# Fewer, longer loads of the combined weights, and two kinds of small transfers moved to GpSimd's queue

## The chip, the core and the metric

The kernel runs on one core of a Trainium2 chip. The metric is the device time of one execution in microseconds (us). Before the change the median of three runs is 834.39 us (834.20 to 834.68).

## What is computed

Eight batches of 576 tokens with eight heads of 64 numbers go through attention inside chunks of 64 tokens, and the 4608 token rows of 512 numbers that come out go through a feed-forward layer with an ELU between its two matrices. Everything is in 32-bit floats.

```python
scores = scale * np.matmul(q_c, k_c.transpose(0, 1, 2, 4, 3))   # chunks of 64
attn = softmax(scores);  out = np.matmul(attn, v_c)
x = out.transpose(0, 2, 1, 3).reshape(B * S, H * D)             # 4608 x 512
h = x @ w_in                                                    # w_in 512 x 2048
g = np.where(h > 0.0, h, np.exp(np.minimum(h, 0.0)) - 1.0)
return g @ w_out                                                # w_out 2048 x 512
```

## The kernel before

**Precision.** An operand is split in a high and a low part, and a product is three matmuls (`three`, L431): high by high, high by low, low by high. Nearly all of PE's time is such 128x512 matmuls at L434.

**Blocks.** The tokens are nine blocks of 512. Blocks 0 to 2 are plain: for each of 16 slices `f` of w_in the first layer (`hidden`), the ELU, the split of its result into `ghi` (ACT) and `glo` (L479, in block 2, the third, on GpSimd), and the second layer. The other six are three superblocks of two blocks, which are multiplied by a scheme of seven products in place of eight. It needs sums and differences of quarters of the weights. Superblock 0 is written out by hand; superblocks 1 and 2 are laid in an order by `Plan`, a list scheduler in the kernel that knows for each job an engine, a time that the engine is occupied, a time until its result can be used, and what it reads and writes.

**Where the combined weights come from.** Those of w_in are made in the second block by `combine` (L512): GpSimd adds, ACT and DVE split, and SP's queue writes the parts to `a_dram` (L536, L537 and L547). Those of w_out are made by the class `Sums` (L564) in eight pieces `j`: GpSimd or DVE adds, ACT makes the high part (`high`), GpSimd or DVE the low one (`low`), and four transfers of 256 KB for each `j` go to `w_dram` (`write_half`, L601). Pieces 4 and 5 are made in the third block (strings such as `w4g` in `MORE_THIRD`; letters g to j are the writes), 0, 3 and 1 in superblock 0, and 2, 6 and 7 (`LATE_SUMS`) at the start of superblock 1.

**The ring.** In superblocks 1 and 2, PE reads the combined weights from a ring of four slots of 512 KB. `load_entry` (L1302) fills a slot when PE is done with the entry four places earlier. A superblock has 28 entries from `a_dram` (its first phase: products with w_in) and then 28 from `w_dram` (second phase). An entry from `a_dram` is two transfers of 256 KB (L1308) in pieces of 1 KB, one from `w_dram` is one transfer of 512 KB (L1313) in pieces of 4 KB. PE uses an entry for two steps of six matmuls. Superblock 0 loads from `a_dram` too (`load_a`, L671).

**Attention beside it.** While a block is multiplied, the attention of a later block is made, one tile of 128 tokens after another. For a tile, PE multiplies q by k (L248, into `ps_a`), DVE and ACT make the softmax, DVE turns blocks of 32x32 (`turned`, L388), ACT copies that to `unturned` (L393), and four transfers of 32 KB exchange the off-diagonal blocks: `swap_turned` (L399) writes parts of `unturned` back into `turned`. Then PE multiplies by v (L256). PE works in order, so a late exchange holds all of its matmuls. Below, an exchange is these four transfers.

**Queues.** Every transfer is issued by SP, in program order: an instruction that waits for its semaphore, or for room in the queue, holds all behind it. GpSimd issues none; it also works in order.

## Time and profile before

| what | value |
|---|---|
| median of three runs | 834.39 us |
| the profiled execution | 837.23 us |
| its span | 835.5 us |
| PE busy | 811.7 us, 97% |
| DVE, ACT, GpSimd busy | 612.4, 523.6 and 165.9 us |
| share of the 16 DMA engines | 77.3%, mean 230 GB/s |
| packets under 2 KB | 195696 of 214335 |

The span is what the trace covers; the profiled execution's own time is 1.7 us longer. Every time on a row counts from the span's start. The profile names a group of instructions by line, engine, operation and tiles (`out<-in`); SPq is SP's queue, and its rows say how long SP took to issue, not how long a transfer ran. "Idle before" in square brackets tells how long the engine stood before a row and who ended that. PE's rows overlap in print, as matmuls are pipelined: what counts is the distance from start to start. Groups of twelve matmuls in stride stand 2.72 us apart.

Stages of the span: plain blocks to about 324 us (the third one from about 233 us), superblock 0 to 506 us, superblock 1 from 506 to 676 us (its first phase to 595 us), superblock 2 from 676 us to the end.

### The profile page before, as it was taken

How to read it: one execution, taken by the hardware profiler on the slowest of the kernel's cores; microseconds unless marked ns; L12 is line 12 of the kernel's file. 1: busy time of each engine (PE TensorE's matmuls, PEld its weight loads, DVE VectorE, ACT ScalarE, POOL GpSimd, SP SyncE). 2: the span in 40 equal slices, each digit the busy share in tenths (PEclk: the TensorE clock that was granted, in tenths of full speed). 3: DMA queues.
4: the chain of work that ended last, by engine and by line, in shares of the span. 5: the costliest groups of instructions: out<-in, count | busy, mean ns of one | idle time of the engine just before them, and what ended most of it. 6: DMA issues, size and time to landing. Idle time of an engine off the chain costs nothing.

```text
span 835.5 us, 15987 instructions
## 1 busy us (share of the span) xinstructions
PE 811.7 (97%) x5853; PEld 660.3 (79%) x5853; DVE 612.4 (73%) x915; ACT 523.6 (63%) x990; POOL 165.9 (20%) x140
## 2 busy tenths in 40 slices
PE   7899999999999989999999999998999999999997
PEld 6688788888878868877888888776788878888886
DVE  4999997666875739766556866867789966557974
ACT  4999875454554535765566445886877736776451
POOL 0000014355335411443111253100020010000100
PEclk8999999999999989999999999999999999999999
DMA  8975764987887887679987898999966587665655
GB/s 232 271 226 192 236 195 138 288 251 252 266 218 212 234 235 196 204 223 252 289 238 216 250 266 284 282 279 265 292 210 204 200 220 228 196 190 197 210 198 152
DMA packets 214335, 191.93 MB, mean 230 GB/s; under 512 B 85616, under 2 KB 195696, under 8 KB 214256
## 3 DMA queue, kind: packets, MB, share of 16 engines
q1 hardware_dynamic: 214256, 190.90, 77.3%
q8 instruction: 47, 0.77, 0.4%
q14 instruction: 32, 0.26, 0.1%
HBM read 144.18 MB, written 42.99 MB: 224 GB/s over the span
## 4 chain that ended last, share of the span: by engine, by line
PE 76%; DMA 8%; ACT 5%; DVE 4%; SPq 4%; issue 2%; POOL 1%; DVEq 0%; POOLq 0%; ACTq 0%
PE o L434 37%; PE h L434 32%; PE ps_a L248 2%; PE ps_a L256 2%; DMA turned<-unturned 2%; DMA ring<-a_dram 2%; DMA kept<-in_q_dram 1%; PE h L451 1%; DMA v_sb<-in_v_dram 1%; SPq L1308 1%; ACT ps_a L1562 1%; DMA g_kept<-lo_dram 1%; SPq L206 1%; DMA ring<-w_dram 1%; DMA q_sb<-in_q_dram 1%
## 5 line engine op out<-in xcount | busy, mean ns | idle before, releaser
L434 PE MATMUL o<-wo_hi,ghi 128*128 128x512 f32 x272 | 108.8, 400 | 0.0
L434 PE MATMUL o<-wo_hi,glo 128*128 128x512 f32 x272 | 107.2, 394 | 0.1
L434 PE MATMUL o<-wo_lo,ghi 128*128 128x512 f32 x272 | 107.1, 394 | 0.0
L434 PE MATMUL h<-xhi,wi_hi 128*128 128x512 f32 x228 | 84.0, 397 | 0.1
L434 PE MATMUL h<-xlo,wi_hi 128*128 128x512 f32 x228 | 82.4, 390 | 0.0
L434 PE MATMUL h<-xhi,wi_lo 128*128 128x512 f32 x180 | 70.3, 390 | 0.0
L434 PEld LDWEIGHTS o<-wo_hi,glo 128*128 128x128 f32 x272 | 51.7, 190 | 11.8 <-DVE glo L479 0.8
L434 PEld LDWEIGHTS o<-wo_hi,ghi 128*128 128x128 f32 x272 | 51.6, 190 | 11.4
L434 PEld LDWEIGHTS o<-wo_lo,ghi 128*128 128x128 f32 x272 | 51.7, 190 | 10.3
L510 POOL TENSOR_TENSOR kept<-wi_hi,wi_lo 128x512 f32<-128x512 f32 x16 | 21.3, 1348 | 158.4 <-DMA kept<-in_k_dram 117.3
L471 DVE SCALAR_TENSOR_TENSOR e<-e,h 128x512 f32<-128x512 f32 x48 | 32.9, 685 | 26.9 <-ACT e L469 26.6
L434 PE MATMUL o<-split,ring 128*128 128x512 f32 x216 | 51.0, 390 | 0.0
L434 PEld LDWEIGHTS h<-xhi,wi_hi 128*128 128x128 f32 x228 | 42.7, 188 | 9.9 <-ACT kept L783 0.7
L434 PEld LDWEIGHTS h<-xlo,wi_hi 128*128 128x128 f32 x228 | 42.9, 188 | 8.5
L434 PEld LDWEIGHTS o<-split,ring 128*128 128x128 f32 x216 | 40.5, 188 | 8.4
L393 ACT COPY unturned<-turned 128x512 f32<-128x512 f32 x28 | 17.4, 622 | 46.7 <-DVE turned L388 45.9
L468 ACT ACTIVATE e<-h 128x512 f32<-128x512 f32 x48 | 28.6, 597 | 28.7 <-PE h L434 26.1
L476 ACT CAST ghi<-e 128x512 fp32r<-128x512 f32 x48 | 29.8, 621 | 18.7 <-DVE e L471 18.6
L434 PE MATMUL h<-split,ring 128*128 128x512 f32 x168 | 40.5, 393 | 0.5 <-DMA ring<-w_dram 0.5
L744 POOL TENSOR_TENSOR glo<-e,ghi 128x512 fp32r<-128x512 f32 x16 | 20.7, 1293 | 99.0 <-ACT ghi L742 99.0
L1488 ACT ACTIVATE e<-e 128x512 f32<-128x512 f32 x64 | 39.5, 630 | 1.0
L434 PEld LDWEIGHTS h<-xhi,wi_lo 128*128 128x128 f32 x180 | 33.8, 188 | 7.1
(224 smaller groups left out, 2014.1 us busy)
## 6 DMA issues: line engine op xcount, KB each, us to landing
ring<-a_dram SPq DMA_DIRECT2D x112, 256.0 KB, 3.9
ring<-w_dram SPq DMA_DIRECT2D x56, 512.0 KB, 3.3
wi_hi<-a_dram SPq DMA_DIRECT2D x56, 256.0 KB, 5.4
kept<-in_q_dram SPq DMA_DIRECT2D x100, 128.0 KB, 3.4
kept<-in_k_dram SPq DMA_DIRECT2D x100, 128.0 KB, 3.9
wo_lo<-lo_dram SPq DMA_DIRECT2D x20, 512.0 KB, 6.1
v_sb<-in_v_dram SPq DMA_DIRECT2D x32, 256.0 KB, 5.4
st<-in_moe_w_in_dram SPq DMA_DIRECT2D x16, 512.0 KB, 4.0
```

Of the source, the lines that this page charges most:

```text
L206: nc.sync.dma_start(out=dst[p0:p0 + n], in_=src[b, :, s0:s0 + n, :].rearrange("h s d -> s h d"))
L248: nc.tensor.matmul(scores[halves[c], j, hp, :], lhsT=qT[halves[j], hp, halves[c]], rhs=kT[halves[j], hp, halves[c]], start=True, stop=True,)
L256: nc.tensor.matmul(x_ps[halves[j], c, hp, :], lhsT=v_sb[halves[c], 2 * hp + j, :], rhs=aT[halves[c], :, j * NK + hp], start=True, stop=True,)
L393: nc.scalar.copy(out=unturned, in_=turned)
L434: nc.tensor.matmul(ps, lhsT=a, rhs=b, start=start, stop=stop, skip_group_check=onto)
L451: nc.tensor.matmul(h, lhsT=w[:, kt, :], rhs=x[:, kt, :], start=i == 0, stop=i == len(terms) - 1)
L468: nc.scalar.activation(out=e, in_=h, func=AF.Relu, scale=-1.0)
L471: nc.vector.scalar_tensor_tensor(out=e, in0=e, scalar=-1.0, in1=h, op0=ALU.add, op1=ALU.max)
L476: nc.scalar.copy(out=ghi, in_=e)
L510: nc.gpsimd.tensor_tensor(out=out, in0=a, in1=b, op=op)
L744: engine.tensor_tensor(out=lo, in0=e, in1=hi.bitcast(F32), op=ALU.subtract)
L1488: nc.scalar.activation(out=units[u], in_=units[u], func=AF.Exp, scale=-1.0)
```

## The change

- `a_dram` is laid out anew, by operand and pair of pieces. An entry of the ring is now one transfer of 512 KB in pieces of 4 KB (56 transfers in place of 112), and a load in superblock 0 has pieces of 2 KB in place of 1 KB. In return `write_parts` issues three transfers of 128 KB in place of one of 256 KB and one of 128 KB (16 more transfers in all), and the pieces of `write_sums` are 1 KB in place of 4 KB.
- The writes of `Sums` pieces 4 and 5 (third block) and 6 and 7 (superblock 1), sixteen transfers of 256 KB, are issued by GpSimd in place of SP. The others stay with SP.
- In the planned part, which is superblock 1, the exchanges are issued by GpSimd: seven of them, 28 transfers. The exchanges of all earlier blocks stay with SP.
- The planner gets a further engine "QUEUE" for what GpSimd issues, with costs of its own, and does not count it as GpSimd's time; `LATE_SUMS` starts pieces 6 and 7 earlier.

```diff
-        def swap_turned(self):
+        def swap_turned(self, queue=nc.sync):
...
-                    nc.sync.dma_start(out=turned[to, 1 - e], in_=unturned[of, e])
+                    queue.dma_start(out=turned[to, 1 - e], in_=unturned[of, e])
...
-    a_dram = dram.tile([NG, P, 2, NA, 2 * P], F32, name="a_dram")
+    a_dram = dram.tile([NA, NG // 2, P, 2, 2, 2 * P], F32, name="a_dram")
...
-            nc.sync.dma_start(out=rows(g, lo)[:, :4], in_=w1.bitcast(F32))
-            nc.sync.dma_start(out=rows(g, lo)[:, 4:6], in_=w2[:, 2:].bitcast(F32))
+            for i, w in enumerate((w1[:, :2], w1[:, 2:], w2[:, 2:])):
+                nc.sync.dma_start(out=rows(i, g, lo), in_=w.bitcast(F32))
...
-                nc.sync.dma_start(out=rows(g, lo)[:, 6:], in_=place_of(g)[:, lo])
+                nc.sync.dma_start(
+                    out=a_dram[3:, g // 2, :, g % 2, lo, :].rearrange("i p w -> p i w"),
+                    in_=place_of(g)[:, lo].rearrange("p (i k) f -> p i (k f)", k=2))
...
-            sums.write_half(lo, half)
+            sums.write_half(lo, half, nc.gpsimd if preparing == "third" else nc.sync)
...
-            for a in range(2):
-                nc.sync.dma_start(
-                    out=slot[:, a].bitcast(F32),
-                    in_=a_dram[2 * d + a, :, :, AOPS.index(PRODUCTS[FIRST[o]][0])])
+            of = a_dram[AOPS.index(PRODUCTS[FIRST[o]][0]), d]
...
+        nc.sync.dma_start(out=slot.bitcast(F32), in_=of)
...
-    LATE_SUMS = (2, 0), (6, 6), (7, 18)
+    LATE_SUMS = (2, 0), (6, 5), (7, 11)
...
-        plan.add(t + 4.7, "SP", dma(4, 420), lambda: later[n].swap_turned(), ["unturned"], ["turned"])
+        plan.add(t + 4.7, "QUEUE", (2400, 4600), lambda: later[n].swap_turned(nc.gpsimd), ["unturned"], ["turned"])
...
+            if early:
+                plan.add(t + .9 + .5 * i, "SP", dma(1, 800), lambda i=i: made[0].write_half(i // 2, i % 2), *keys)
+            else:
+                plan.add(t + 1.5 + 4 * i, "QUEUE", (2400, 5000),
+                         lambda i=i: made[0].write_half(i // 2, i % 2, nc.gpsimd), *keys)
```

**SP in the third block**, from one exchange to the next (the second is the one at 288.56 us of the profile). Before:

```order
L399 DMA turned<-unturned 32x256 x4
L671 DMA wi_hi<-a_dram 128x2x256 x2
L227 DMA kept<-in_q_dram 32x4x256 x4
L227 DMA kept<-in_k_dram 32x4x256 x4
L601 DMA w_dram<-io 128x2x256
L687 DMA wo_lo<-lo_dram 128x1024
L671 DMA wi_hi<-a_dram 128x2x256 x2
L601 DMA w_dram<-io 128x2x256
L206 DMA v_sb<-in_v_dram 128x8x64
L399 DMA turned<-unturned 32x256 x4
```

After:

```order
L399 DMA turned<-unturned 32x256 x4
L673 DMA wi_hi<-a_dram 128x512 x2
L227 DMA kept<-in_q_dram 32x4x256 x4
L227 DMA kept<-in_k_dram 32x4x256 x4
L689 DMA wo_lo<-lo_dram 128x1024
L673 DMA wi_hi<-a_dram 128x512 x2
L206 DMA v_sb<-in_v_dram 128x8x64
L399 DMA turned<-unturned 32x256 x4
```

The two writes of `io` (piece 4's sums, issued at 284.94 and 287.12 us) that stood between the exchanges are gone from SP. On GpSimd each now stands directly behind a `glo`, those that ran at 272.71 and 278.07 us before, with no loads in front of it.

**SP in the first phase of superblock 1**, where the ring is loaded, from the second exchange to the third. Before:

```order
L399 DMA turned<-unturned 32x256 x4
L1308 DMA ring<-a_dram 128x2x256 x4
L227 DMA kept<-in_k_dram 32x4x256 x2
L1308 DMA ring<-a_dram 128x2x256 x2
L227 DMA kept<-in_k_dram 32x4x256 x2
L206 DMA v_sb<-in_v_dram 64x8x64 x2
L1308 DMA ring<-a_dram 128x2x256 x2
L227 DMA kept<-in_q_dram 32x4x256 x4
L1308 DMA ring<-a_dram 128x2x256 x2
L227 DMA kept<-in_k_dram 32x4x256 x2
L1308 DMA ring<-a_dram 128x2x256 x2
L227 DMA kept<-in_k_dram 32x4x256
```

After, from the same loads of k on:

```order
L227 DMA kept<-in_k_dram 32x4x256 x2
L1313 DMA ring<-a_dram 128x1024
L227 DMA kept<-in_k_dram 32x4x256 x2
L1313 DMA ring<-a_dram 128x1024
L206 DMA v_sb<-in_v_dram 64x8x64 x2
L227 DMA kept<-in_q_dram 32x4x256
L1313 DMA ring<-a_dram 128x1024
L227 DMA kept<-in_q_dram 32x4x256 x3
L227 DMA kept<-in_k_dram 32x4x256
L1313 DMA ring<-a_dram 128x1024
L227 DMA kept<-in_k_dram 32x4x256 x3
L1313 DMA ring<-a_dram 128x1024 x5
```

The exchanges have left SP's queue, and each entry is one row where it was two.

**GpSimd at the start of superblock 1** (`g_more` holds pieces 6 and 7, `split` low parts for the second phase). Before:

```order
L589 TENSOR_TENSOR g_kept<-g_kept 128x256
L589 TENSOR_TENSOR g_more<-g_more 128x256
L574 TENSOR_TENSOR g_more<-wo_hi,wo_lo 128x512
L589 TENSOR_TENSOR g_more<-g_more 128x256 x3
L1752 TENSOR_TENSOR split<-g_kept,split 128x512 x3
```

After:

```order
L591 TENSOR_TENSOR g_kept<-g_kept 128x256
L591 TENSOR_TENSOR g_more<-g_more 128x256 x5
L603 DMA w_dram<-g_more 128x2x256 x2
L1752 TENSOR_TENSOR split<-g_kept,split 128x512
L603 DMA w_dram<-g_more 128x2x256
L399 DMA turned<-unturned 32x256 x4
L603 DMA w_dram<-g_more 128x2x256 x3
L1752 TENSOR_TENSOR split<-g_kept,split 128x512
L603 DMA w_dram<-g_more 128x2x256 x2
L1752 TENSOR_TENSOR split<-g_kept,split 128x512
L399 DMA turned<-unturned 32x256 x12
```

The first exchange now stands behind three writes and a split on GpSimd, the second behind five more writes and two splits; between the later ones little is left.

More of the change, by code (lines that the diff above doesn't have):

```diff
@@ L529, in sums, with rows @@
             pool(s3, a11, a21, ALU.subtract)
-        def rows(g, lo):
-            return a_dram[g, :, lo].rearrange("p i (k f) -> p (i k) f", k=2)
+        def rows(i: int, g: int, lo: int):
+            return a_dram[i, g // 2, :, g % 2, lo].rearrange("p (k f) -> p k f", k=2)
         def write_parts(g, lo):
             w1, w2 = w_in_slices(2 * g)[lo], w_in_slices(2 * g + 1)[lo]
-            nc.sync.dma_start(out=rows(g, lo)[:, :4], in_=w1.bitcast(F32))
-            nc.sync.dma_start(out=rows(g, lo)[:, 4:6], in_=w2[:, 2:].bitcast(F32))
+            for i, w in enumerate((w1[:, :2], w1[:, 2:], w2[:, 2:])):
+                nc.sync.dma_start(out=rows(i, g, lo), in_=w.bitcast(F32))
         def split(g):
@@ L597, in low, with write_half @@
                 op=ALU.subtract)
-        def write_half(self, lo: int, half: int):
+        def write_half(self, lo: int, half: int, queue=nc.sync):
             of = slice(2 * half, 2 * half + 2)
-            nc.sync.dma_start(
+            queue.dma_start(
                 out=w_dram[of, self.j // 2, :, self.j % 2, lo, :].rearrange("i p w -> p i w"),
@@ L672, in load_a @@
             out=a_place(i - 1).bitcast(F32).rearrange("p (l a) -> p l a", l=2),
-            in_=a_dram[g % NG, :, :, AOPS.index(name)])
+            in_=a_dram[AOPS.index(name), g // 2, :, g % 2])
     def a_operand(i: int):
@@ L895, in order @@
             jobs, done = self.jobs, []
-            free = {"PE": 0.0, "ACT": 2600.0, "DVE": 2600.0, "POOL": 0.0, "SP": 3500.0}
+            free = {"PE": 0.0, "ACT": 2600.0, "DVE": 2600.0, "POOL": 0.0, "SP": 3500.0, "QUEUE": 0.0}
             port, moved = {"DVE": 0.0, "POOL": 0.0}, [0.0]
@@ L944, in order @@
                 nexts, some = [], False
-                for e in ("PE", "SP", "ACT", "DVE", "POOL"):
+                for e in ("PE", "SP", "ACT", "DVE", "POOL", "QUEUE"):
                     i, when = choice(e, now)
@@ L1306, in load_entry @@
             d, o = divmod(e, 7)
-            for a in range(2):
-                nc.sync.dma_start(
-                    out=slot[:, a].bitcast(F32),
-                    in_=a_dram[2 * d + a, :, :, AOPS.index(PRODUCTS[FIRST[o]][0])])
+            of = a_dram[AOPS.index(PRODUCTS[FIRST[o]][0]), d]
         else:
             o, d = divmod(e, PAIRS)
-            nc.sync.dma_start(out=slot.bitcast(F32), in_=w_dram[W_OPS.index(SECOND[o]), d])
+            of = w_dram[W_OPS.index(SECOND[o]), d]
+        nc.sync.dma_start(out=slot.bitcast(F32), in_=of)
     def summed(e: int):
@@ L1622, in add_entry @@
     def add_entry(t: float, e: int):
-        plan.add(t, "SP", dma(1 if e % ENTRIES >= 7 * PAIRS else 2, 1650), lambda: load_entry(e),
+        plan.add(t, "SP", dma(1, 1600), lambda: load_entry(e),
                  [("sums", j) for j in summed(e)], [("ring", e % 4)])
@@ L1900, in add_sums @@
         for i in range(4):
-            plan.add(t + .9 + .5 * i, "SP", dma(1, 800), lambda i=i: made[0].write_half(i // 2, i % 2),
-                     place[i // 2 * 2:i // 2 * 2 + 2], [("sums", j)])
+            keys = place[i // 2 * 2:i // 2 * 2 + 2], [("sums", j)]
+            if early:
[3 more added lines that the diff above has]
+                         lambda i=i: made[0].write_half(i // 2, i % 2, nc.gpsimd), *keys)
     for j, t in LATE_SUMS:
```

## The prediction

> **What bounds the kernel now.** PE is busy for 811.7 of 835.5 us, so I look for the places where it does not run in stride. I read first the stages (windows), then PE's timeline for idle time, then SP's queue and the DMA engines in the stage that loses most, then the chain at the largest single stall.
>
> The windows are superblock 1's two phases; both hold 336 matmuls on the ring. Columns: the window, its length, busy time of PE, PEld, DVE, ACT, POOL with counts, PE's clock, DMA share, GB/s.
>
> ```profile
> 506.44:595.30 88.86, 84.46 (x593) 65.79 (x591) 67.54 (x109) 71.34 (x172) 11.83 (x8) 1.00 0.91 273
> 595.30:676.45 81.15, 81.15 (x560) 66.52 (x561) 73.40 (x123) 54.14 (x131) 10.36 (x7) 1.00 0.68 215
> ```
>
> The first phase takes 7.7 us more. One attention score more (0.6 us) is in it, so about 7.1 us are lost. Its DMA share is 0.91 against 0.68. PE's timeline there shows who ended the waits:
>
> ```profile
> 540.01 2.98 PE L434 MATMUL o<-t_place,ring 128*128 128x512 f32 x12 [0.42 <-DMA ring<-a_dram]
> ...
> 545.41 1.65 PE L434 MATMUL o<-xlo,ring 128*128 128x512 f32 x6 [1.06 <-ACT spare L1464]
> ...
> 565.11 3.00 PE L434 MATMUL o<-xlo,ring 128*128 128x512 f32 x12 [0.27 <-DMA ring<-a_dram]
> 569.14 2.99 PE L434 MATMUL h<-xhi,ring 128*128 128x512 f32 x12 [1.04 <-DMA ring<-a_dram]
> ...
> 582.55 3.01 PE L434 MATMUL o<-wo_lo,ring 128*128 128x512 f32 x12 [0.92 <-DMA ring<-a_dram]
> ...
> 595.30 3.06 PE L434 MATMUL h<-split,ring 128*128 128x512 f32 x12 [0.48 <-DMA ring<-w_dram]
> ```
>
> Five waits for the ring, 3.1 us in print; the print undercounts, as from 565.11 to 569.14 twelve matmuls take 4.03 us, 1.3 over the 2.72 of the stride, where only 1.04 are shown. I put the ring at 4.3 of the 7.1 us, ACT at 1.4, and the rest to restarts. Why does the ring come late? SP's queue at this place (start, time to issue):
>
> ```profile
> 566.61 1.18 SPq L1308 DMA_DIRECT2D ring<-a_dram  x2
> 567.84 0.59 SPq L227 DMA_DIRECT2D kept<-in_k_dram  x1
> 568.52 2.48 SPq L399 DMA_DIRECT2D turned<-unturned  x4
> 571.10 2.94 SPq L1308 DMA_DIRECT2D ring<-a_dram  x4
> 574.09 0.59 SPq L227 DMA_DIRECT2D kept<-in_k_dram  x1
> ```
>
> SP issues without a pause; an exchange holds the ring's next load for 2.5 us, and an entry takes two issues of 0.59 us. So two things are short: SP's time and the DMA engines.
>
> The largest single stall is in the third block. PE's timeline, two tiles of attention:
>
> ```profile
> 280.23 0.69 PE L248 MATMUL ps_a<-k_turned,qT 64*64 64x64 f32 x32
> ...
> 284.18 0.39 PE L434 MATMUL h<-xhi,wi_hi 128*128 128x512 f32 x1
> ...
> 292.46 0.69 PE L248 MATMUL ps_a<-k_turned,qT 64*64 64x64 f32 x32
> 296.03 1.50 PE L256 MATMUL ps_a<-turned,v_sb 64*64 64x64 f32 x32 [2.87 <-issue]
> ...
> 302.61 0.39 PE L434 MATMUL h<-xhi,wi_hi 128*128 128x512 f32 x1
> ```
>
> From the scores to the next first layer (two attention products and twelve matmuls) the earlier tile takes 3.95 us, this one 10.15: 6.2 us lost. The chain of waits says how:
>
> ```profile
> 288.56 6.33 DMA turned<-unturned
> ...
> 297.52 5.25 PE o L434 x12
> 302.77 2.74 PE h L434 x12
> ```
>
> The exchange took 6.33 us from issue to landing, and after the wait twelve matmuls took 5.25 in place of 2.72 us: the wait of 2.87 us cost the clock, too. Waits of 1.0 us (569.14 above) were followed by 2.99 us for twelve, nearly stride.
>
> **The change part by part.**
>
> *A, superblock 1, first phase.* Off SP: four exchanges of 2.48 us, one of two issues of 0.59 us for each of 28 entries (16.5 us), and eight writes at about 0.6 us: some 31 of 88.9 us of a queue without pause. The DMA engines gain as well. Two stretches of superblock 2 have almost nothing but the ring, 700 to 740 us in pieces of 1 KB and 770 to 820 us in pieces of 4 KB (packets, MB, share):
>
> ```profile
> q1 hardware_dynamic: 7982, 7.70, 69.0%
> ...
> q1 hardware_dynamic: 4759, 10.12, 62.3%
> ```
>
> That is 2.79 against 3.25 GB/s for each per cent of share, so an entry costs 14% less. The 28 entries (14.7 MB in 88.9 us, 165 GB/s) take 59 points of the 91 now, and 8 less after. With both SP and the engines below their limit, as in the second phase, I take the ring's 4.3 us as gone. ACT's 1.4 us and the restarts stay: ACT is busy for 71.3 us, which would be 88% of an unstalled phase.
>
> What comes in is the exchange on GpSimd. What it may take is the time from `unturned` to PE's product with v. Rows of ACT and PE for the first two tiles:
>
> ```profile
> 528.88 0.61 ACT L393 COPY unturned<-turned 128x512 f32<-128x512 f32 x1
> ...
> 547.64 0.60 ACT L393 COPY unturned<-turned 128x512 f32<-128x512 f32 x1
> ```
>
> ```profile
> 534.64 0.66 PE L256 MATMUL ps_a<-turned,v_sb 64*64 64x64 f32 x32
> ...
> 555.69 0.65 PE L256 MATMUL ps_a<-turned,v_sb 64*64 64x64 f32 x32
> ```
>
> That leaves 5.15 us for the first and 7.45 for the second, of which some 2.5 are PE's own stalls that go: about 5 us each. Nothing in the trace shows a transfer issued by GpSimd. From below: SP's 0.62 us for each of four, and the shortest landing, 1.8 us, make 4.3. From above: four times 1.29 us, an ordinary GpSimd operation (row of part B), and the longest landing, 6.3, make 11.5.
>
> ```profile
> DMA to landing us min/median/max: 1.8/2.8/6.3
> ```
>
> I take SP's issue and the median landing, 5.3 us, as it is the same transfer with the same descriptors: 0.2 and 0.3 us late. On GpSimd it also waits in order: three writes and a split stand ahead of the first exchange, so I add 0.3, together 0.8 us. A = 4.3 - 0.8 = 3.5 us gained. Bounds: 7.1 gained if ACT's waits go too, nothing or a loss if exchanges are slow (below).
> The Trainium skill, page "DMA: Bandwidth & Descriptors", section "Latency and other measured facts", has the first byte at about 1 us for GpSimd's transfers against 0.6 us for SP's. No row here shows it; four in series would be 1.6 us later, 3.2 on two tight tiles, and the sum below would come to 829.7.
>
> *B, the third block's stall.* SP's rows in front of the exchange:
>
> ```profile
> 284.94 0.38 SPq L601 DMA_DIRECT2D w_dram<-io  x1
> ...
> 287.12 0.60 SPq L601 DMA_DIRECT2D w_dram<-io  x1
> 287.82 0.64 SPq L206 DMA_DIRECT2D v_sb<-in_v_dram  x1
> 288.56 4.15 SPq L399 DMA_DIRECT2D turned<-unturned  x4
> ```
>
> ```profile
> 286.96 0.62 ACT L393 COPY unturned<-turned 128x512 f32<-128x512 f32 x1 [1.23 <-DVE turned L388]
> ```
>
> `unturned` was ready at 287.6. Without the two writes (1.2 us with their gaps) SP can issue at 287.6 in place of 288.56. The issue took 4.15 in place of 2.48 us, as the queue was full; 512 KB fewer just ahead is 2 us of transfers at the 240 GB/s of this stretch (last number of its window; the one before is the engines' share):
>
> ```profile
> 280.00:303.00 23.00, 20.13 (x192) 16.18 (x191) 13.64 (x22) 10.04 (x17) 6.22 (x4) 0.85 0.89 240
> ```
>
> PE could take v at 293.0, and did at 296.0. Of that 3.0 us I take off 1.0 and most of 1.7: about 0.6 us of wait stays, short of what cost the clock. With a restart of 1.1 us, B = 6.2 - 1.7 = 4.5 us. Bounds: 0 to 6.2.
> The cover for the writes on GpSimd is its idle time ahead of each `glo`, the least where a write comes in:
>
> ```profile
> 278.07 1.29 POOL L479 TENSOR_TENSOR glo<-e,ghi 128x512 fp32r<-128x512 f32 x1 [1.16 <-ACT ghi L476]
> ```
>
> ```profile
> 281.89 0.40 PE L434 MATMUL o<-wo_hi,glo 128*128 128x512 f32 x1
> ```
>
> That `glo` ends 2.5 us before PE needs it, so a write may hold GpSimd for 1.16 + 2.5 = 3.7 us at no cost. Beyond that each write delays PE.
>
> *C, superblock 0.* Pieces of 2 KB for 56 loads, 256 KB each; PE shows one wait for an exchange of 0.77 us there (at 389.24). I take 0.4 gained; bounds 0 and 0.8.
>
> ```profile
> 389.24 1.03 PE L256 MATMUL ps_a<-turned,v_sb 64*64 64x64 f32 x32 [0.77 <-DMA turned<-unturned]
> ```
>
> *D, start of superblock 2.* PE waits 1.10 us for the fifth entry behind three groups of four output transfers:
>
> ```profile
> 688.59 2.97 PE L434 MATMUL h<-t_place,ring 128*128 128x512 f32 x12 [1.10 <-DMA ring<-a_dram]
> ```
>
> The new order puts eight of them ahead of the third entry, which is due 5.4 us after the superblock's start; SP's 4.8 us for eight (0.6 each) leave little for the load. I take 0.5 lost (bounds: 1.1 gained, 1.5 lost).
>
> *E, second block.* Sixteen more issues, 0.6 us each, and pieces of 1 KB in `write_sums`. PE has no idle row there; nothing, at worst 1 us.
>
> Sum: -3.5 - 4.5 - 0.4 + 0.5 = -7.9 us. The profiled execution is 837.2 with 835.5 in its span, 1.7 us outside that do not change; the median of the runs is 834.4, 2.8 us below the profiled one, and the stalls should be the same in both. 834.4 - 7.9 = 826.5.
>
> **The rivals.**
>
> *R1, the burst stays.* The two writes leave SP's queue but not the engines: if GpSimd issues them while the third block's loads run, the exchange still lands late, and only A and C come, less D: 834.4 - 3.4 = 831.0. For: the stretch runs at 0.89 of the engines' share. Against: on GpSimd they stand behind `glo`s at 272.7 and 278.1, before the crowd. The Trainium skill, page "DMA: Bandwidth & Descriptors", section "Issuing engines are not separate DMA queues", speaks for it: another issuing engine saves only issue time. Chance 0.14.
>
> *R2, the wait changes its name.* ACT at 88% and the exchanges hold PE in superblock 1 as long as the ring did, and B is cut only to its 1.0 us of earlier issue, which D's upper end takes back: 834.4. Chance 0.09.
>
> *R3, slower: exchanges on GpSimd come too late.* If each takes 9.4 us (four issues of 1.29 and the landing of 4.2 that exchanges had between 545 and 590 us), the four tiles of the first phase are late by about 4.3 us each, 17.2 in all, against 9.2 gained (ring, B and C) and 0.5 lost (D): 842.9. It decides from 7.3 us for an exchange, where four times 2.2 take all.
>
> ```profile
> turned<-unturned SPq DMA_DIRECT2D x9, 32.0 KB, 4.2
> ```
>
> For it: GpSimd's work can be held by DVE, as here, three times an ordinary operation's time:
>
> ```profile
> 514.50 3.87 POOL L574 TENSOR_TENSOR g_more<-wo_hi,wo_lo 128x512 f32<-128x512 f32 x1
> ```
>
> Against: what is held there reads SBUF; a transfer's issue need not. The Trainium skill, page "SBUF — State Buffer", section "Who interferes with whom", lets only DVE's copies, casts and tensor_scalar hold GpSimd's descriptor writing, and infers that its tensor_tensor does not; DVE's work in this phase is nearly all of the latter kind, so by that rule R3 is unlikely. Chance 0.15.
>
> **How the numbers follow.** Forecast 0.62, R1 0.14, R2 0.09, R3 0.15. The forecast's own range goes from 819 (A 7.1, B 6.2, C 0.8, D 1.1) to 831 (A 1.5, B 2.5, rest as summed). With R1 and R2 it reaches to 836; R3 and a tenth of the forecast stay out. A measurement tells 0.2%, 1.7 us, from no change: below 832.7 is faster, above 836.1 slower. Forecast and R1 are faster (0.76), R2 is mostly the same (0.08), R3 and a rest of R2 slower (0.16).
>
> **What would show it.** Right: the first phase of superblock 1 takes about 85 us, its DMA share falls to 0.85 or less, PE's waits for `ring<-a_dram` are gone, SP's queue has pauses; the row of 2.87 us is gone and its twelve matmuls take 2.7 us. Wrong: PE waits at L256 for `turned` in superblock 1 by over 2 us a tile (R3), at L434 for `glo` in the third block, or the stall near 296 us stands as it was (R1).

## The result and the profile after

The changed kernel takes 842.6 us (median of four runs, 838.48 to 845.52), the kernel before 834.3 us in the runs beside it (832.53 to 834.68). The ratio is 1.0099, with a 95% interval of 1.0076 to 1.0123: 1% slower. The forecast was 826.5, and the range of 819 to 836 does not hold the result. It lies where rival R3 put it (842.9), though not by the mechanism that R3 argued.

The profiled execution of after took 842.35 us, its span is 840.6. First the windows of superblock 1's two phases (columns as in the prediction):

```profile
501.24:598.89 97.65, 87.65 (x594) 70.67 (x592) 66.86 (x107) 70.11 (x170) 25.40 (x33) 0.93 0.85 259
598.89:679.86 80.97, 80.97 (x561) 66.41 (x560) 74.23 (x124) 54.93 (x133) 16.30 (x19) 1.00 0.63 199
```

The first phase starts 5.2 us earlier than before and then takes 97.65 us in place of 88.86. The share of the DMA engines is 0.85 for 0.91, as forecast, but only because the phase is longer: share times length is 83.0 us after and 80.9 before. PE's granted clock is 0.93 in place of 1.00. PE's timeline there, around the first two tiles of attention, shows where:

```profile
535.65 0.44 PE L256 MATMUL ps_a<-turned,v_sb 64*64 64x64 f32 x2 [4.61 <-DMA turned<-unturned]
536.39 1.13 PE L256 MATMUL ps_a<-turned,v_sb 64*64 64x64 f32 x30 [0.30 <-DMA turned<-unturned]
537.45 5.54 PE L434 MATMUL o<-wo_lo,ring 128*128 128x512 f32 x18
542.83 2.88 PE L434 MATMUL o<-t_place,ring 128*128 128x512 f32 x12
...
561.17 1.52 PE L256 MATMUL ps_a<-turned,v_sb 64*64 64x64 f32 x32 [3.96 <-DMA turned<-unturned]
562.62 5.16 PE L434 MATMUL h<-wo_lo,ring 128*128 128x512 f32 x12
567.62 2.91 PE L434 MATMUL o<-wo_lo,ring 128*128 128x512 f32 x12
```

PE waits 4.61 + 0.30 and 3.96 us for the exchange, 8.9 in all. After the first wait 18 matmuls take 5.38 us from start to start where the stride (twelve in 2.72) gives 4.08; after the second twelve take 5.00. The granted clock was 0.50 to 0.51 from 535.6 to 540.0 us and 0.50 to 0.56 from 561.0 to 567.6. With the products by v, which are slower too, the clock costs some 5 us more. Of the ring's waits, which the change was to take away, one of 0.43 us is left in this phase. In part that is the lateness itself, which gives the ring time: in the kernels layout and swap_sp below, in which PE waits for no exchange, the ring's waits are 2.3 and 2.7 us.

Why is the exchange late? ACT's rows say when `unturned` was ready, 522.91 and 549.76 us:

```profile
522.31 0.60 ACT L393 COPY unturned<-turned 128x512 f32<-128x512 f32 x1
...
549.16 0.60 ACT L393 COPY unturned<-turned 128x512 f32<-128x512 f32 x1
```

GpSimd's timeline, with the idle time ahead of each row:

```profile
514.17 0.72 POOL L603 DMA_DIRECT2D w_dram<-g_more  x1
520.67 0.73 POOL L603 DMA_DIRECT2D w_dram<-g_more  x1 [5.78 <-DMA v_sb<-in_v_dram]
521.43 1.30 POOL L1752 TENSOR_TENSOR split<-g_kept,split 128x512 fp32r<-128x512 f32 x1
527.89 0.72 POOL L603 DMA_DIRECT2D w_dram<-g_more  x1 [5.16 <-issue]
528.61 2.02 POOL L399 DMA_DIRECT2D turned<-unturned  x4
...
548.70 0.73 POOL L603 DMA_DIRECT2D w_dram<-g_more  x1 [4.64 <-issue]
555.20 0.73 POOL L603 DMA_DIRECT2D w_dram<-g_more  x1 [5.77 <-DVE g_kept L1491]
555.95 1.29 POOL L1752 TENSOR_TENSOR split<-g_kept,split 128x512 fp32r<-128x512 f32 x1
557.17 2.03 POOL L399 DMA_DIRECT2D turned<-unturned  x4
```

The exchanges are issued 5.7 and 7.4 us after their source was ready. Ahead of each stands a write that itself stood idle for over 5 us. The names in the brackets change from row to row, and twice it is "issue", a wait for nothing that the profile shows. The group of DMA issues between 500 and 700 us gives the median landing of such a write:

```profile
w_dram<-g_more POOLq DMA_DIRECT2D x8, 256.0 KB, 6.2
```

The same view of one write at a time tells when each landed (us; the rows at 535.25, 538.62 and 542.01 are among those left out above):

| write issued | landed after | that is at | next write issued |
|---|---|---|---|
| 514.17 | 6.2 | 520.4 | 520.67 |
| 520.67 | 6.9 | 527.6 | 527.89 |
| 527.89 | 7.0 | 534.9 | 535.25 |
| 535.25 | 3.0 | 538.3 | 538.62 |
| 538.62 | 3.1 | 541.7 | 542.01 |
| 542.01 | 6.4 | 548.4 | 548.70 |
| 548.70 | 6.2 | 554.9 | 555.20 |

Each write goes out 0.3 to 0.4 us after the one ahead of it has landed, whether that took 3 us or 7.

In the third block the change did what it was to do. SP's exchange there, which took 4.15 us to issue before, and PE's product with v:

```profile
289.52 2.45 SPq L399 DMA_DIRECT2D turned<-unturned  x4
```

```profile
294.91 1.10 PE L256 MATMUL ps_a<-turned,v_sb 64*64 64x64 f32 x32
```

The wait of 2.87 us is gone: this row has none. At the start of superblock 2 the new order costs more than forecast. PE's timeline, and SP's queue ahead of it:

```profile
687.47 3.00 PE L434 MATMUL h<-wo_lo,ring 128*128 128x512 f32 x12 [2.01 <-DMA ring<-a_dram]
...
693.56 2.96 PE L434 MATMUL h<-t_place,ring 128*128 128x512 f32 x12 [0.36 <-DMA ring<-a_dram]
```

```profile
677.97 4.45 SPq L1641 DMA_DIRECT2D out_dram<-g_kept  x8
682.52 0.99 SPq L1313 DMA_DIRECT2D ring<-a_dram  x2
```

Eight output transfers stand ahead of the third entry, and PE waits 2.01 + 0.36 us where it waited 1.10.

The 5.1 us between the two spans, by starts of PE's rows (before to after): the start-up to the scores (L248) at 146.29 / 147.14 us costs 0.85, and the change touches nothing there; the second block and the start of the third, to the scores at 280.23 / 281.84, 0.76; three tiles of the third block, to 323.08 / 320.08, gain 4.61; superblock 0 gains 2.20; superblock 1's first phase costs 8.79; its second phase gains 0.18; superblock 2 costs 1.69. The sum is +5.1.

### The profile page after: what moved, and what is told of

Its sections match the earlier page's. It is cut to its first block, busy times and chain, and to the rows that moved or that the text cites. A ratio compares the mean times of both kernels' runs of the same rounds, so it can differ in the third digit from the quotient of the medians.

```text
span 840.6 us, 15885 instructions
## 1 busy us (share of the span) xinstructions
PE 810.9 (96%) x5853; PEld 660.4 (79%) x5853; DVE 614.4 (73%) x914; ACT 523.3 (62%) x990; POOL 194.2 (23%) x185
## 4 chain that ended last, share of the span: by engine, by line
PE 72%; DMA 10%; DVE 5%; SPq 5%; issue 4%; ACT 3%; POOL 1%; DVEq 0%; ACTq 0%; POOLq 0%
PE o L434 36%; PE h L434 31%; DMA turned<-unturned 2%; PE ps_a L256 2%; SPq L206 2%; PE ps_a L248 2%; DMA kept<-in_q_dram 1%; DMA ring<-a_dram 1%; SPq L652 1%; DMA g_kept<-lo_dram 1%; DMA io<-in_k_dram 1%; SPq L399 1%; DMA st<-in_moe_w_in_dram 1%; DMA a_dram<-wi_hi 1%; ACT e L468 1%
## 5 line engine op out<-in xcount | busy, mean ns | idle before, releaser
L510 POOL TENSOR_TENSOR kept<-wi_hi,wi_lo 128x512 f32<-128x512 f32 x16 | 24.7, 1562 | 157.6 <-DMA kept<-in_k_dram 118.1
L434 PEld LDWEIGHTS o<-wo_lo,ghi 128*128 128x128 f32 x272 | 51.1, 188 | 10.3
```

Source lines behind the costliest of these rows:

```text
L434: nc.tensor.matmul(ps, lhsT=a, rhs=b, start=start, stop=stop, skip_group_check=onto)
L510: nc.gpsimd.tensor_tensor(out=out, in0=a, in1=b, op=op)
```

## The experiments

Theory **T1**: a write of 256 KB on GpSimd's queue cannot be issued before the write ahead of it has landed, since the room for its descriptors (the entries that are written for a transfer; `dynamic_dma_scratch_size` in the kernel sets the room) is too small; GpSimd stands still meanwhile, and the exchange, in order behind the writes, is late. The rivals to it are R3 as the prediction argued it (an exchange issued by GpSimd is late by itself, through VectorE or through slow issues), and that the new layout or the ring makes PE late. Each kernel has 12 runs (layout_third: 11), with runs of before on the same chip: median 834.20 us for the first four kernels, 832.94 for the next four, 833.17 for the last. Single runs of one kernel spread over 5 to 9 us, so only the ratios are compared.

**1. More room for descriptors (ring2048).** After, with one number changed:

```diff
-                     dynamic_dma_scratch_size=512)
+                     dynamic_dma_scratch_size=2048)
```

> The changed kernel with four times the space for GpSimd's transfer descriptors (2048 in place of 512 bytes of a partition), nothing else. Theory T1 (a 256 KB write on GpSimd's queue has to wait until the write before it has landed, as there is room for one only, and the exchange stands behind it): the pauses of 2.6 to 5.8 us ahead of the writes go, exchanges are issued within 1 us of `unturned`, PE's waits of 4.6 and 4.0 us at L256 go with their clock loss of about 5 us: about 829 us. Rival T2 (an exchange issued by GpSimd is slow in itself in a crowded stage: 2.0 us to issue and up to 6 us to land): the first two waits shrink by less than half, 838 us or more.

835.19 us, ratio 1.0027 (1.0002 to 1.0051). The group of the late writes in after (count, nanoseconds, first and last start) and in this kernel:

```profile
L603 POOL DMA_DIRECT2D w_dram<-g_more x8: 725/730/752, 514.2 to 555.2; - x8
```

```profile
L603 POOL DMA_DIRECT2D w_dram<-g_more x8: 727/727/752, 512.4 to 532.4; - x8
```

Eight writes are out in 20 us in place of 41, with the same issue time each. GpSimd's exchange follows its copy, ready at 521.2 us, at once:

```profile
521.51 2.12 POOL L399 DMA_DIRECT2D turned<-unturned  x4 [0.83 <-ACT unturned L393]
523.62 2.21 POOL L603 DMA_DIRECT2D w_dram<-g_more  x3
```

PE waits for no exchange in superblock 1. So the waits are T1's, but the time is 6 us above the 829 that T1 gave. PE waits for the ring again, five times and 3.9 us in the first phase; that the writes, now issued closer together, meet the ring's loads is argued. The longest:

```profile
542.09 2.97 PE L434 MATMUL o<-xhi,ring 128*128 128x512 f32 x12 [1.36 <-DMA ring<-a_dram]
```

**2. The late writes back on SP, the exchanges on GpSimd (late_sp).** After, with

```diff
-            if early:
+            if True:
                 plan.add(t + .9 + .5 * i, "SP", dma(1, 800), lambda i=i: made[0].write_half(i // 2, i % 2), *keys)
```

> The changed kernel with the writes of pieces 6 and 7 back on SP's queue; the exchanges stay on GpSimd, now with no write ahead of them. T1: no wait at L256 over 1 us, SP's queue somewhat fuller: about 829 us. T2: waits for `turned` of 2 us and more stay: 838 us or more. Rival T3 (in this stage the exchanges are late for `unturned` itself, by ACT): the exchanges are issued as late as in the changed kernel.

831.31 us, ratio 0.9967 (0.9945 to 0.9988). Nothing stands ahead of the exchange, which GpSimd issues 0.3 us after its copy (ready at 522.0 us); of PE's waits for `turned` 2.6 us are left of 8.9. One of them, 1.18 us, is longer than T1 allowed, and the time is 2 us above its 829:

```profile
522.35 2.04 POOL L399 DMA_DIRECT2D turned<-unturned  x4 [5.38 <-ACT unturned L393]
```

```profile
528.65 0.30 PE L256 MATMUL ps_a<-turned,v_sb 64*64 64x64 f32 x2 [0.94 <-DMA turned<-unturned]
529.46 0.69 PE L256 MATMUL ps_a<-turned,v_sb 64*64 64x64 f32 x30 [0.52 <-DMA turned<-unturned]
...
550.15 0.69 PE L256 MATMUL ps_a<-turned,v_sb 64*64 64x64 f32 x30 [1.18 <-DMA turned<-unturned]
```

**3. The exchanges back on SP, the late writes on GpSimd (swap_sp).** After, with

```diff
-        plan.add(t + 4.7, "QUEUE", (2400, 4600), lambda: later[n].swap_turned(nc.gpsimd), ["unturned"], ["turned"])
+        plan.add(t + 4.7, "SP", dma(4, 420), lambda: later[n].swap_turned(), ["unturned"], ["turned"])
```

> The changed kernel with the exchanges back on SP's queue; the writes of pieces 6 and 7 stay on GpSimd. T1: the writes still wait for each other (pauses of 3 to 6 us on GpSimd stay), but nothing that PE needs soon stands behind them: about 830 us. T2: the same time, as the slow exchanges are gone; T2 and T1 differ in whether GpSimd's pauses ahead of writes stay with no exchange among them (T1: yes).

832.83 us, ratio 0.9988 (0.9967 to 1.0008). GpSimd still stands still ahead of its writes, with no exchange on its queue:

```profile
530.17 0.73 POOL L603 DMA_DIRECT2D w_dram<-g_more  x1 [4.82 <-DVE g_kept L1491]
537.80 0.73 POOL L603 DMA_DIRECT2D w_dram<-g_more  x1 [6.90 <-issue]
```

But nothing urgent is behind them, and PE has no wait for `turned` in superblock 1. So each move without the other is harmless, and the loss is of the two together: after 1.0099, either part taken back 0.9967 or 0.9988. Without the late writes on GpSimd after would be some 11 us faster, without its exchanges there some 9. The pauses are T1's here too: the write of 530.17 landed after 7.3 us, at 537.5, and the next was issued at 537.80.

**4. The layout alone (layout).** After, with all writes and exchanges on SP and the late sums where they were in before:

```diff
-            sums.write_half(lo, half, nc.gpsimd if preparing == "third" else nc.sync)
+            sums.write_half(lo, half)
...
-    LATE_SUMS = (2, 0), (6, 5), (7, 11)
+    LATE_SUMS = (2, 0), (6, 6), (7, 18)
```

and the two edits of 2 and 3.

> Only the new layout of a_dram with one load per entry; all transfers on SP, the old LATE_SUMS. If the layout is what I took it for, superblock 1's first phase loses 3 to 4 us less than before, and the third block's stall may stay (its writes are back on SP): 828 to 832 us. Rival T4 (the layout itself costs, by its shorter pieces in the second block or at the start of superblock 2): 836 us or more.

832.85 us, ratio 0.9983 (0.9963 to 1.0004). The time is just above the 828 to 832 that the expectation gave. The layout does not make the loss, and gains little. Its first phase is short (86.53 us), and the third block's stall is gone here too, with the writes still on SP: the exchange that took 4.15 us to issue in before takes 2.89, 0.02 us after its copy. The loads of 256 KB around it have pieces of 2 KB now in place of 1 KB, and take SP 0.34 us each to issue in place of 0.59 (rows at the end); that this is the reason is argued. SP's queue, and ACT's copy:

```profile
289.37 2.89 SPq L399 DMA_DIRECT2D turned<-unturned  x4
```

```profile
288.72 0.63 ACT L393 COPY unturned<-turned 128x512 f32<-128x512 f32 x1 [1.23 <-DVE turned L388]
```

**5. The planner told the true cost (true_cost).** After, with the time that a write holds GpSimd's queue set to what the trace shows:

```diff
-                plan.add(t + 1.5 + 4 * i, "QUEUE", (2400, 5000),
+                plan.add(t + 1.5 + 4 * i, "QUEUE", (6500, 7000),
```

> The changed kernel, whose planner is told that a write by GpSimd holds its queue for 6.5 us (the landing of 6.2 us in the changed kernel's trace) instead of 2.4. The plan then puts the first two exchanges of superblock 1 behind two writes each instead of three and more. Theory T1 (each write waits for the landing of the one ahead, and the exchange stands behind the writes): an exchange issues within 2 us of its copy, the matmuls of x wait for turned by less than 2 us a tile instead of 4.9 and 4.0, and the time falls by most of the 8 us lost: 832 to 836. Rival T2 (an exchange issued by GpSimd is late by itself, since VectorE holds GpSimd or its descriptors take long): the order among GpSimd's own instructions changes little, the two waits stay at 4 to 5 us, 840 or more.

837.92 us, ratio 1.0048 (1.0024 to 1.0072). The first two exchanges now stand behind two writes each and are issued 0.3 us after their copies, and PE's waits for `turned` in superblock 1 are 1.9 us in all. That is T1's mark. The time is above what T1 was to give, for a reason that I had not seen: the second piece's four writes still come at the pace of one in 6 us, and the tile that they read is wanted again. GpSimd's third of the four, DVE's next write of that tile, and PE's wait:

```profile
559.43 0.72 POOL L603 DMA_DIRECT2D w_dram<-g_more  x1 [5.19 <-issue]
```

```profile
565.26 0.69 DVE L1467 TENSOR_TENSOR g_more<-h,kept 128x512 f32<-128x512 f32 x1 [2.51 <-DMA w_dram<-g_more]
```

```profile
571.40 2.93 PE L434 MATMUL h<-xhi,ring 128*128 128x512 f32 x6 [3.73 <-DVE g_more L1467]
```

The third write landed after 5.7 us, at 565.1. DVE's next write of `g_more` waits for that, and PE waits 1.03 and 3.73 us for DVE. The order on the queue decides who is late, not how fast the writes go.

**6. The layout and the third block's writes (layout_third).** As layout, but with the third-block writes on GpSimd as in after.

> The new layout and the first superblock's third-block writes on GpSimd; the late sums' writes, their places in the plan and the exchanges as before. If the third block's stall near 296 us is what SP's crowded queue costs, and GpSimd's writes there take it away (step B of the prediction), this is faster than the layout alone (832.85) by 3 to 6 us: 827 to 830. Rival: the stall of 6.2 us in the profile of before belongs to that one execution, and the writes on GpSimd there are worth nothing: 831 to 834, and no wait over 1 us at the gather's or the scores' matmuls of the third block in either trace.

829.62 us, ratio 0.9957 (0.9932 to 0.9982). The interval overlaps that of layout (0.9983), so it does not show what the writes add beside the layout, and the third block is as short in both traces (37.84 and 38.02 us in the table below). The rival, that the stall belonged to one execution, is answered by the next kernels.

**7. Both moves without the layout (old_layout_late_sp).** As late_sp, but with `a_dram` and its loads and writes as in before.

> The fast variant found so far (late sums' writes on SP, exchanges and third-block writes on GpSimd; 831.3) with the old layout of a_dram and two loads per w_in entry. If the larger pieces and the single loads carry the gain in the first phase (prediction A, 5.2 us before superblock 1 and 4.3 us of ring waits), ring waits of 0.4 us and more return there and the time is 3 to 5 us above it: 834 to 836. Rival: SP has been relieved enough by the four exchanges that left it, and the layout is worth nothing: 830 to 832.

829.42 us, ratio 0.9943 (0.9919 to 0.9967), no worse than late_sp with the new layout. My expectation fell, and the rival stands: what the layout gains in one stage it gives back in others (the table below).

**8. Before once more (before_again).**

> The kernel before once more, for a second profile of it and for what two equal kernels show against each other: ratio 1.000 within 0.003. If the third block's stall near 296 us belongs to the kernel, the row with a wait of some 2.9 us ahead of the gather's or the scores' matmul stands in this trace too and the span is again about 835; if it belonged to that execution, it is gone and the span is 828 to 832.

833.52 us, ratio 0.9987 (0.9964 to 1.0009). The third block's stall is in it, as two waits, and SP's exchange is slow again:

```profile
293.18 0.29 PE L256 MATMUL ps_a<-turned,v_sb 64*64 64x64 f32 x2 [1.39 <-DMA turned<-unturned]
294.44 0.69 PE L256 MATMUL ps_a<-turned,v_sb 64*64 64x64 f32 x30 [0.96 <-DMA turned<-unturned]
```

```profile
286.45 4.46 SPq L399 DMA_DIRECT2D turned<-unturned  x4
```

So the stall belongs to the kernel.

**9 to 11. One part at a time, on before (third_only, exch_only, third_exch).** Before, with the third-block writes on GpSimd; with the exchanges of the planned part on GpSimd and the planner's engine QUEUE for them; with both. The edits are those of the change:

```diff
-            sums.write_half(lo, half)
+            sums.write_half(lo, half, nc.gpsimd if preparing == "third" else nc.sync)
...
-        plan.add(t + 4.7, "SP", dma(4, 420), lambda: later[n].swap_turned(), ["unturned"], ["turned"])
+        plan.add(t + 4.7, "QUEUE", (2400, 4600), lambda: later[n].swap_turned(nc.gpsimd), ["unturned"], ["turned"])
```

> The kernel before with one part of the change: the third-block writes of superblock 0 issued by GpSimd, layout, late sums and exchanges as before. The new layout with these writes gave 829.62 (ratio 0.9957), the layout alone 832.85 (0.9983). If the gain is that of these writes (SP's queue is relieved by them, prediction step B, though the stall of 6.2 us itself stood in one execution only), the ratio is 0.995 to 0.998. Rival: the gain needs the larger pieces, and this reads 1.000 within 0.003.

> The kernel before with one part of the change: the four later exchanges issued by GpSimd, which has no writes then. Theory T1 (the exchange was late through the writes ahead of it): each exchange is issued within 1 us of its copy, the matmuls of x wait for turned by less than 2 us a tile, and SP's freed 2.5 us an exchange bring the ring loads forward: ratio 0.995 to 0.999. Rival R3 as the prediction argued it (VectorE holds GpSimd or its descriptors, an exchange of 9.4 us by itself): waits of 4 us and more a tile, ratio 1.008 to 1.012.

> The two parts together: the third-block writes and the exchanges on GpSimd, the layout and the late sums as before. If the parts add up, the ratio is the product of the two single ones, 0.991 to 0.996 and 826 to 830 us; if one is worth nothing beside the other, it is that of the better one.

third_only: 830.44 us, ratio 0.9968 (0.9951 to 0.9986), as expected, though its expectation still took the stall for that of one execution. Eight writes moved to an idle queue gain 0.3%, and the exchange there is issued in 2.48 us again:

```profile
286.88 2.48 SPq L399 DMA_DIRECT2D turned<-unturned  x4
```

exch_only: 833.20 us, ratio 0.9998 (0.9977 to 1.0019). Neither side's numbers came: no waits of 4 us, and no gain. The exchange is issued 0.3 us after its copy, and lands late all the same. GpSimd's and PE's rows for the first tile, and the whole group:

```profile
528.53 2.11 POOL L399 DMA_DIRECT2D turned<-unturned  x4 [5.34 <-ACT unturned L393]
```

```profile
535.84 0.69 PE L256 MATMUL ps_a<-turned,v_sb 64*64 64x64 f32 x30 [1.76 <-DMA turned<-unturned]
```

```profile
L399 POOL DMA_DIRECT2D turned<-unturned x28: 496/496/636, 528.5 to 650.2; - x28
```

From the first issue to the product are 7.3 us, of which 2.1 are the four issues. Before has no wait for `turned` in this phase; here it is 0.49 + 1.76 us. The ring's waits, which SP's spared time was to shorten, are 3.5 us in print, against 3.1 in before and 3.7 in before_again. third_exch: 830.70 us, ratio 0.9959 (0.9942 to 0.9977), that is third_only's gain; the exchanges add nothing that can be told.

**12. A second dose of room (ring1024).** As ring2048 with 1024.

> The changed kernel with 1024 bytes for GpSimd's descriptors instead of 512 (with 2048 it took 835.19, ratio 1.0027). Theory T1 by a second dose: two writes have room, so a write is issued without a pause if the one before its predecessor has landed; the first exchange of superblock 1 stands behind three writes and is 0 to 3 us late instead of 5.7, the waits for turned sum to 0 to 4 us instead of 8.9, and the time lies between the two: 833 to 839. Rival: the room is not what makes the writes wait (the pauses are those of VectorE's port or of the source tiles), and this stays at 840 or more.

832.83 us, ratio 0.9989 (0.9964 to 1.0014). The eight writes take 20 us from the first start to the last (517.2 to 537.3), as with 2048, and PE has no wait for `turned` in superblock 1. So the step lies between 512 and 1024 bytes. The landings tell how many writes are under way at once. The fourth goes out at 528.33, before the second and the third have landed (529.2 and 530.9); the fifth (529.43) goes out 0.3 us after the second's landing, the sixth (531.24) 0.3 us after the third's. That is three, where 512 bytes let one go; the expectation had two. The time came out just below what T1 gave, and the rival (840 or more) fell.

**The stages of all kernels.** Each part of the change touches some stages only, so a stage can be compared across all kernels that share its code. The table gives distances between starts of PE's rows: from the scores (L248) near 146 us to those near 280 us; from there over three tiles; from there to the first matmul on the ring; the first phase of superblock 1; and from superblock 2's first ring matmul to the end of the span.

| kernel | second block, start of the third | third block | superblock 0 | first phase | superblock 2 |
|---|---|---|---|---|---|
| before | 133.94 | 42.85 | 183.36 | 88.86 | 159.05 |
| before_again | 133.49 | 41.06 | 182.38 | 90.42 | 158.42 |
| exch_only | 134.37 | 42.83 | 181.64 | 89.01 | 158.87 |
| third_only | 133.89 | 37.11 | 181.28 | 89.95 | 158.95 |
| third_exch | 133.71 | 38.33 | 182.02 | 87.85 | 159.34 |
| old_layout_late_sp | 133.75 | 38.32 | 181.13 | 89.52 | 158.83 |
| layout | 136.12 | 38.02 | 181.14 | 86.53 | 158.96 |
| layout_third | 135.87 | 37.84 | 181.13 | 86.46 | 159.15 |
| swap_sp | 136.67 | 38.06 | 181.19 | 86.00 | 160.01 |
| late_sp | 135.51 | 37.41 | 181.21 | 86.66 | 160.44 |
| ring2048 | 136.12 | 37.64 | 181.17 | 87.76 | 161.54 |
| ring1024 | 138.56 | 37.67 | 181.15 | 87.18 | 161.87 |
| true_cost | 137.01 | 37.49 | 181.16 | 92.13 | 160.75 |
| after | 134.70 | 38.24 | 181.16 | 97.65 | 160.74 |

The upper six have the old layout, the others the new one. The second phase of superblock 1 is not in the table: it takes 81.0 to 81.2 us in all fourteen. Each row is one profiled execution, and some of these lie up to 4 us off the median of their kernel: layout 829.37 us (median 832.85), swap_sp 829.28 (832.83), ring1024 836.81 (832.83). The first column spreads from 134.70 to 138.56 us over kernels with the same code in it, the fourth differs by 1.6 us between two profiles of before. So the table tells where time goes; how much a kernel gains is told by its ratio. By the profiles layout is 7.9 us faster than before, by the runs 1.4.

## Why the prediction was wrong, point by point

**A, superblock 1's first phase: the step that failed.** The prediction put it as: "three writes and a split stand ahead of the first exchange, so I add 0.3". I had counted the writes as issues, about as long as SP's 0.6 us. With this room each one holds GpSimd until its predecessor has landed (the table of landings, experiments 1, 3 and 12), and the two exchanges behind them are late by 5.7 and 7.4 us. The whole lateness was put at 0.8 us. In the table of stages it is 97.65 less 86.33, the mean of the three kernels that have the new layout and SP's exchanges: 11.3 us, in PE's waits and in the slow matmuls behind them. By the runs it is 11 us as well (after against late_sp). The order on the queue was seen; that the queue may have a limit of its own was not, and no bound was put on how long a write holds it.

The other half of A came in part. With the new layout and SP's exchanges the first phase takes 86.33 us on average, with the old one 89.74 (before, before_again, third_only): 3.4 us gained in these profiles, of the 4.3 that I gave the ring's waits. But those waits have not gone: they are 2.0 to 2.7 us in print with the new layout, 3.1 to 4.5 with the old one. And the DMA engines were not relieved. Layout's window of the phase:

```profile
501.14:587.67 86.53, 83.59 (x593) 66.15 (x592) 67.89 (x110) 71.66 (x173) 11.84 (x8) 1.00 0.96 284
```

Its share is 0.96 where 0.85 or less was the sign, and share times length is 83.2 us on average in the three kernels of either layout. The 8 points that I took off for larger pieces do not show. That the 3.4 us come from SP's halved issues is argued: in exch_only SP is spared the exchanges, and the ring's waits stay. The smaller steps: GpSimd's issue of 0.50 us for a transfer of an exchange came out a little below SP's 0.62; the landing of 2.8 us was too short: it is a median over all exchanges, where the group of GpSimd's 28 in exch_only has 4.7. By the starts of issue and product, those on which PE waited took 7.3 us (exch_only), 7.1 and 8.5 (late_sp, from 522.35 and 541.65 us), not 5.3. The prediction had a nearer row, the 4.2 us of R3, and used it only for the rival.

**R3** gave the time, 842.9, and the sign that the prediction named for it is there: PE waits at L256 by more than 2 us, though at two of the phase's four tiles. But its reason was not the cause. With no writes on GpSimd the exchange follows its copy by 0.3 us, and all 28 issues take 496 to 636 ns, beside a DVE that is busy for 69.86 of the 89.01 us of this phase in exch_only. The Trainium skill, page "SBUF — State Buffer", section "Who interferes with whom", infers that DVE's tensor_tensor does not hold GpSimd's descriptor writing; these rows agree. The prediction calls DVE's work there nearly all of that kind; by the rows of before's window it is about half, the rest is mostly scalar_tensor_tensor and transposes, and under 2 us are copies and tensor_scalar. The 9.4 us were made up of the wrong parts: the delay lay ahead of the first issue, not in the four issues. R3 had four tiles late by 4.3 us each; two were, by 4.9 and 4.0, and the slow clock behind them made up the rest. That the time agrees is luck.

**B, the third block.** Forecast 4.5 us gained, measured 4.4 in the profiles: the mean of the three kernels with the stall is 42.25 us (before, before_again, exch_only), that of the other eleven 37.8. The stall stands in each of the three traces that have SP's writes and the old layout, and GpSimd's writes alone take it away (third_only, 0.9968; by its runs 2.7 us, 1.2 to 4.1). What I did not see is that the new layout alone does so as well, so the two parts do not add up. That the queue was full, as the prediction has it, no row shows. R1, in which the burst stays, fell. The cover for the writes held: in the whole of after PE shows one wait for `glo`, of 0.23 us, and that in the second block; the third block's writes go out 5.4 us apart and more.

**C, superblock 0.** Forecast 0.4 gained; 181.1 to 181.2 us with the new layout against a mean of 182.0 with the old one (181.1 to 183.4), 0.8 gained. It is 2.2 between the two profiles of the result; two profiles of before differ by 1.0, so the size is not clear.

**D, the start of superblock 2.** Forecast 0.5 lost (bound 1.5). The place was right: in seven of the eight kernels with the new layout PE waits there for the first time at the third entry, by 0.9 to 2.2 us (in true_cost at the fourth, by 1.1; in swap_sp the row names ACT and not the ring), in none with the old layout. The size was too small: the mean of the last column is 158.9 us with the old layout, 159.1 with layout and layout_third, and 160.9 with the six others that have the new one. So 2.0 are lost in after's kind of plan, with its places for the late sums; why layout, with the same wait, loses next to nothing stays open.

**E, the second block.** Forecast nothing, at worst 1 us. Means of the first column: 133.9 and 136.3 us, 2.5 lost (0.8 between the two profiles of the result). Part of it is in SP's queue at the end of the block. In before the exchange near 239 us is issued as soon as ACT is done, in layout 1.7 us later, with the rows of ACT and of SP for each, before first:

```profile
238.69 0.62 ACT L393 COPY unturned<-turned 128x512 f32<-128x512 f32 x1 [2.70 <-DVE turned L388]
```

```profile
239.33 2.48 SPq L399 DMA_DIRECT2D turned<-unturned  x4
```

```profile
239.19 0.62 ACT L393 COPY unturned<-turned 128x512 f32<-128x512 f32 x1 [2.70 <-DVE turned L388]
```

```profile
241.49 2.71 SPq L399 DMA_DIRECT2D turned<-unturned  x4
```

That SP is behind by the sixteen added issues, or by the smaller pieces of `write_sums`, is argued, not shown: no kernel changed one of the two alone.

**The sum.** With the measured sizes A without the lateness, B, C, D and E give -3.4 - 4.4 - 0.8 + 2.0 + 2.5 = -4.1 us, about half of the forecast's -7.9. By the runs late_sp, which is after without the lateness, gains 2.8 us (1.0 to 4.6). The lateness of 11.3 makes the sum +7.2; measured are +8.3 (6.3 to 10.3 by the interval). R2, no change, fell as well. The versions that beat both kernels are third_only (0.9968, one edit), third_exch, layout_third, late_sp and old_layout_late_sp (0.9943). Their intervals overlap; all five have the third block's writes on GpSimd, and none has the late ones there.

## What to carry to other kernels

Before a queue gets its first work, ask what it can hold, not only what an issue costs: a transfer that has to wait for room, as GpSimd's writes did here, stops its engine, and all that stands in order behind it. Small urgent transfers and large patient ones may each go to a quiet queue, but not to the same one while it has room for one write. And a change of several parts is best read by stages: here four stages that moved by 1 to 4 us in both directions lay beside an effect of 11.

## What the runs showed of the hardware

- **Room for GpSimd's descriptors.** With 512 bytes, a 256 KB write is issued 0.3 to 0.4 us after the landing of the one ahead (eight in 41 us, median landing 6.2 us). With 1024 bytes three are under way at once; with 1024 and with 2048 the eight take 20 us. The issue itself is 0.73 us for 256 KB and 0.50 us for 32 KB.
- **Issue time by piece size on SP.** A load of 256 KB in the third block takes SP longer in pieces of 1 KB (third_only, first row) than of 2 KB (layout, second row; nanoseconds, shortest, median, longest):

```profile
L671 SPq DMA_DIRECT2D wi_hi<-a_dram x7: 523/592/610, 277.1 to 295.9; - x7
```

```profile
L673 SPq DMA_DIRECT2D wi_hi<-a_dram x7: 319/344/581, 279.5 to 298.8; - x7
```

- **PE's clock after a wait.** Waits of 4.6 and 4.0 us in after were followed by a granted clock of 0.50 to 0.56 for 4 and 7 us. But so was one of 2.87 us in before (0.50 from 296.0 to 300.0 us) and one of 1.82 us in ring2048 (0.50 from 678.0 to 680.6), while after 2.01 us in after it stayed at 1.00 (the row of 687.47 above):

```profile
676.38 4.48 PE L434 MATMUL h<-wo_lo,ring 128*128 128x512 f32 x12 [1.82 <-DMA ring<-a_dram]
```

The Trainium skill, page "TensorE: Matmul & The Clock Gate", section "Part 1: The HAM clock gate (the "warmup" mystery)", has the clock halve after an idle window of about 3.4 us. The two long waits agree; the half clock after 2.87 and 1.82 us does not follow from it, and where the measurement differs it decides. No run here tells what else is needed.
